# Attention and mixture-of-depths on one core: batch 2 loaded ahead of the expert weights, scatter-adds and row stores later, and matmuls of zeros at the start

## The chip, the cores and the metric

The kernel runs on one core of a Trainium2 chip. The metric is the device time of one execution in microseconds. Before the change it is 253.89 us, the median of three runs (253.05 to 253.95). The profiled execution took 251.56 us, of which 249.8 us lie between its first and its last instruction; every position in time below is counted from that first instruction.

## The reference

Two stages, for 8 batches of 448 tokens. The first is attention with a squared relu in place of the softmax, over 12 heads of 64. The second takes the 128 tokens of each batch with the highest gate score, runs them through an expert of two matrices, and adds the gated result to their rows.

```python
scores = q @ k.T / sqrt(64)                    # per batch and head, 448 x 448
x      = (maximum(scores, 0)**2 / 448) @ v     # heads side by side: 448 x 768
s      = x @ w_gate                            # per batch, 448
top    = indices of the 128 largest s
h      = maximum(x[top] @ w1, 0)               # 768 -> 1024
out    = x;  out[top] += sigmoid(s[top]) * (h @ w2)
```

Inputs and output are in fp32. Each batch of q, k and v is 4.13 MB in memory and 2.06 MB on the chip, as the loads cast to bf16.

## The kernel before

**The stages of a pair.** Work goes by pairs of heads: 8 batches of 6 pairs, 48 iterations of one loop. (b, p) is the iteration for pair p of batch b. `transposes` brings q and k of a pair into the layout that the scores need (TensorE, then a copy `qkt` by VectorE). `scores` makes four chunks of the score matrix (L186, L190), `relu` evacuates each on ScalarE (L198), `square` squares it on VectorE (L204), and `attend` multiplies by v (L214). `evacuate` writes the transposed output of the pair to `xT`, on VectorE for pairs 0, 4 and 5 and on ScalarE for the others; a DMA transpose on the SyncE queue (L229) then turns it into the columns of `x_sb`, the rows of the batch. Iteration (b, p) does the transposes of the *next* pair and attends to and evacuates the *previous* one, so the transposes for pair 0 of batch b+1 are in (b, 5), and `attend` for the last pair of batch b is in (b+1, 0).

**The expert, in the shadow of later batches.** Tables (`PE`, `ACT`, `DVE`, `DVE2`) place its steps. In batch b's iterations the tokens of batch b-1 are ranked: gate scores at pair 0, `rank_chunk` (L280) from pair 2, the one-hot matrix `hot` at pair 4, and `gather` (L296) at pair 5. One iteration later, at (b+1, 0), `chosen` writes the row indices `idx` (L306) and the gate `g`, and `gathered` copies the tokens to `xeT`. In batch b+1's iterations the expert of batch b-1 runs: `hidden` (w1, L329) at pairs 0 to 2, `project` (w2, L345) at pairs 3 and 4, `gated` (L350) writes `gye` at pairs 4 and 5. So `idx` of batch b is written at (b+2, 0), and `gye` of batch b is complete at (b+2, 5).

**Buffers.** q, k and v have three sets of buffers, used in turn: load b overwrites what batch b-3 used. `x_sb`, `idx` and `gye` have two: `idx` of batch b+2 is written over that of batch b, which the scatter-add of batch b must have read by then; `x_sb` of batch b+2 is written over that of batch b, which its store must have read.

**The order on the queues.** The loop stands in a manual schedule: each engine works its instructions off in the order in which the loop writes them. The loads, the weights, the row stores (L233) and the scatter-adds (L384) are all DMAs issued by GpSimd, one after the other on one queue, and GpSimd stands still while one of them waits to be issued. A load of a batch is nine DMAs: one for q and four each for k and v. There are eight completion semaphores for these DMAs, used in turn, so each waits at its issue for the landing of the one eight places ahead of it. The store of a batch covers rows of `out` and the scatter-add addresses all of `out`, so a scatter-add waits for the landing of a store issued ahead of it, and a store for that of a scatter-add ahead of it.

Before the change, GpSimd issues load 0, load 1, the four iotas (from which VectorE makes `slot_row`, `tie` and `tok`), w1, w2 and load 2. Then, with load(b+2) at (b, 0), the store of batch b-1 when its last pair is evacuated at (b, 0), and the scatter-add of batch b-2 at (b, 5), the order is: load 3, store 0, load 4, store 1, scatter-add 0, load 5, store 2, scatter-add 1, load 6, store 3, scatter-add 2, load 7, store 4, scatter-add 3, and from there a store and a scatter-add in turn.

Of the kernel before, what the change touches and what calls it, by code (L numbers as in the profile page):

```python
# [7 lines left out]
FP32 = mybir.dt.float32  # L8
BF16 = mybir.dt.bfloat16
# [10 lines left out]
def kernel(  # L20
# [11 lines left out]
    nc = tc.nc  # L32

    B, H, S, Dh = q.shape
# [43 lines left out]
    def load_q(b, h0, h1):  # L78
        nc.gpsimd.dma_start(
            out=q_sb[b % NBUF][:, h0:h1],  # L80
            in_=q[b, h0:h1].rearrange("h (p c) d -> p h c d", c=NC))
# [13 lines left out]
    def load(b, h0, h1):  # L95
        load_q(b, h0, h1)
        load_kv(k_sb, k, b, h0, h1)
        load_kv(v_sb, v, b, h0, h1)


    load_q(0, 0, 2)
    wg_cols = const.tile([128, NM], FP32)
    nc.sync.dma_start(out=wg_cols, in_=moe_w_gate.rearrange("(m p) -> p m", p=128))
# [11 lines left out]
    for i in range(1, NBUF):  # L115
        zero_halves(i)
    load(1, 0, H)
    w1_sb = const.tile([128, NM, F], BF16)
    w2_sb = const.tile([128, NF, HD], BF16)

    wg_rep = const.tile([128, NM, 128], BF16)
    nc.vector.tensor_copy(out=wg_rep,
# [26 lines left out]
        nc.vector.tensor_copy(out=t[:, :, 0:2], in_=tok_i)  # L149
        tok.append(t)  # L150

    nc.gpsimd.dma_start(out=w1_sb, in_=moe_w1.rearrange("(m p) f -> p m f", p=128))
    nc.gpsimd.dma_start(out=w2_sb, in_=moe_w2.rearrange("(m p) f -> p m f", p=128))


    qkt, s_ps, a_sb, o_ps, x_sb = {}, {}, {}, {}, {}
# [61 lines left out]
    def evacuate(t):  # L218
        b, hp = divmod(t, NHP)
        xt = xT[b % 2][:, hp, :, :P]  # L220
        o = o_ps.pop(t).rearrange("d (c p) -> d c p", p=P)
        if hp in (0, 4, 5):
            nc.vector.tensor_scalar(out=xt, in0=o, scalar1=o_scale, scalar2=None, op0=ALU.mult)  # L223
        else:
            nc.scalar.activation(out=xt, in_=o, func=AF.Copy, scale=o_scale)
        if hp == 0:
            x_sb[b] = x_pool.tile([128, NC, HD], BF16, name="x_sb")

        nc.sync.dma_start_transpose(  # L229
            out=x_sb[b][:, :, hp * 128:(hp + 1) * 128],  # L230
            in_=xT[b % 2][:, hp].rearrange("d c p -> d (c p)"))
        if hp == NHP - 1:
            nc.gpsimd.dma_start(out=out[b].rearrange("(p c) d -> p c d", c=NC), in_=x_sb[b][:P])  # L233

# [85 lines left out]
    def moe_ffn(b, idx, g, xeT):  # L320
        hT = moe_pool.tile([128, NF, CAP], BF16, name="hT")
        gye = moe_pool.tile([CAP, HD], FP32, name="gye")
        ps = {}

        def hidden(f, pool=mb_ps_pool, tag="m"):
            if f % 4 == 0:
                ps["h", f // 4] = pool.tile([128, 4, CAP], FP32, name="h_ps", tag=tag)
            for m in range(NM):
                nc.tensor.matmul(out=ps["h", f // 4][:, f % 4, :],  # L329
                                 lhsT=w1_sb[:, m, f * 128:(f + 1) * 128],  # L330
                                 rhs=xeT[:, m, :], start=(m == 0), stop=(m == NM - 1))

        def hidden_relu(i):
            nc.scalar.activation(out=hT[:, 4 * i:4 * i + 4, :], in_=ps["h", i], func=AF.Relu)

        def sigmoid():
            nc.scalar.activation(out=g, in_=g, func=AF.Sigmoid)

        def project(half, f0, f1, pool=None, tag="m"):
            cols_d = slice(half * 384, half * 384 + 384)  # L340
            if f0 == 0:
                pool = pool or (ma_ps_pool, mb_ps_pool)[half]
                ps["y", half] = pool.tile([CAP, 384], FP32, name="ye_ps", tag=tag)
            for f in range(f0, f1):
                nc.tensor.matmul(out=ps["y", half], lhsT=hT[:, f, :], rhs=w2_sb[:, f, cols_d],  # L345
                                 start=(f == 0), stop=(f == NF - 1))

        def gated(half):
            cols_d = slice(half * 384, half * 384 + 384)
            nc.scalar.activation(out=gye[:, cols_d], in_=ps["y", half], func=AF.Copy,  # L350
                                 scale=g[:, 0:1])
            if half == 1:
                scatter()

        def last():

            nc.scalar.activation(out=g, in_=g, func=AF.Sigmoid)
            for half in range(2):
                h = s_ps_pool.tile([128, 4, CAP], FP32, name="h_ps2", tag="s")
                for m0 in (0, 3):  # L360
                    for ff in range(4):
                        f = 4 * half + ff
                        for m in range(m0, m0 + 3):
                            nc.tensor.matmul(out=h[:, ff, :],
                                             lhsT=w1_sb[:, m, f * 128:(f + 1) * 128],
                                             rhs=xeT[:, m, :], start=(m == 0 and ff == 0),
                                             stop=(m == NM - 1), skip_group_check=True)
                f = 4 * half
                nc.scalar.activation(out=hT[:, f:f + 4, :], in_=h, func=AF.Relu)
            y = [mb_ps_pool.tile([CAP, 384], FP32, name="y_ps2", tag="m"),  # L370
                 t_ps_pool.tile([CAP, 384], FP32, name="y_ps3", tag="t")]
            for f0 in (0, 4):
                for half in range(2):
                    for f in range(f0, f0 + 4):
                        nc.tensor.matmul(out=y[half], lhsT=hT[:, f, :],
                                         rhs=w2_sb[:, f, half * 384:half * 384 + 384],
                                         start=(f == 0), stop=(f == NF - 1))
            nc.scalar.activation(out=gye[:, :384], in_=y[0], func=AF.Copy, scale=g[:, 0:1])
            nc.vector.tensor_scalar(out=gye[:, 384:], in0=y[1], scalar1=g[:, 0:1],
                                    scalar2=None, op0=ALU.mult)  # L380
            scatter()

        def scatter():
            nc.gpsimd.indirect_dma_start(  # L384
                out=out.rearrange("b s d -> (b s) d"),
                out_offset=bass.IndirectOffsetOnAxis(ap=idx[:, :1], axis=0),
                in_=gye, in_offset=None, element_offset=b * S * HD, compute_op=ALU.add)

        return {"h": hidden, "hT": hidden_relu, "sig": sigmoid, "y": project, "gye": gated,
                "last": last}  # L390


# [42 lines left out]
    with tc.manual_schedule():  # L435
        transposes(0)
        for t in range(NT):
            b, hp = divmod(t, NHP)
            scores(t, 0)
            scores(t, 1)  # L440
            relu(t, 0)
            relu(t, 1)
            moe(ACT, b, hp)
            if t > 0:
                square(t - 1, 3)
            moe(DVE, b, hp)
            if t + 1 < NT:
                transposes(t + 1)
            if t > 0:
                attend(t - 1)  # L450
                if hp not in (0, 1, 5):
                    evacuate(t - 1)
            if hp == 0 and b + 2 < B:
                load(b + 2, 0, H)
            scores(t, 2)
            relu(t, 2)
            square(t, 0)
            if t > 0 and hp in (0, 1, 5):
                evacuate(t - 1)
            square(t, 1)  # L460
            moe(DVE2, b, hp)
            scores(t, 3)
            relu(t, 3)
            square(t, 2)
            moe(PE, b, hp)
        square(NT - 1, 3)
        place(ACT, B - 1, NHP)
        place(DVE, B - 1, NHP)
        last, prev = B - 1, B - 2
        r, handed[last] = moe_rank(last)  # L470
        f = moe_ffn(prev, *handed.pop(prev))
        attend(NT - 1)
        evacuate(NT - 1)
        r["gate"](0, NM - 1)
        for i in range(4):
            f["h"](i)
        r["gate"](NM - 1, NM)
        f["hT"](0)
        r["bc"]()
        for i in range(4, 8):  # L480
            f["h"](i, t_ps_pool, "t")
        r["col"]()
        r["pieces"]()
        for c in range(NC):
            r["rank"](c)
        r["hot"]()
        f["hT"](1)
        f["sig"]()
        f["y"](0, 0, 8, mb_ps_pool)
        f["y"](1, 0, 8, o_ps_pool, "o")  # L490
        f["gye"](0)
        f["gye"](1)
        r["xe"](0, t_ps_pool, "t")
        r["sel"]()
        r["xe"](1, ma_ps_pool)
        r["xeT"](0)
        r["xeT"](1)
        r["chosen"]()
        moe_ffn(last, *handed.pop(last))["last"]()
# [33 lines left out]
```

## Time and profile before

| what | value |
|---|---|
| time, median of 3 | 253.89 us |
| span of the profiled execution | 249.8 us, mean granted TensorE clock 0.942 |
| TensorE / VectorE / ScalarE busy | 201.2 / 179.9 / 183.2 us |
| GpSimd's DMA queue (loads, weights, stores, scatter-adds) | 40768 packets, 33.82 MB, 84.4% of the span of 16 engines |
| SyncE's DMA queue (48 transposes) | 26896 packets, 6.30 MB, 25.2% |
| scatter-adds, from issue to landing | 5.5 to 7.0 us |
| row stores, from issue to landing | 5.2 to 15.7 us |
| w1, w2, from issue to landing | 17.3 and 26.1 us |

The profile's slices give the busy share of each engine in 40 equal parts of the span, in tenths. In the timelines a row is a group of instructions: start, length, engine, line, operation, what it writes and reads, and, in brackets, how long the engine had been idle before it and what ended that. The releaser is inferred from semaphores: where an instruction waits for several things, the one that came last by the profile is named. "Issue to landing" of a DMA begins when the engine issues it; it includes the time that it stands in its queue behind others. A packet's share of time includes its waiting, so the two queues together can exceed 100%.

### The profile page before, as it was taken

The numbers are of one execution on the slowest core, as the hardware profiler recorded it, in microseconds if no ns is written. First come the engines' busy times: TensorE is split into PE (matmuls) and PEld (weight loads), VectorE is DVE, ScalarE is ACT, GpSimd is POOL, SyncE is SP. The second block draws the span as 40 slices with busy tenths as digits, with TensorE's granted clock in tenths as the row PEclk, the third lists the DMA queues.
The fourth block names the chain that finished last, engine by engine and source line by source line (L and its number), as shares of the span: only waits on it lengthen the run. The fifth ranks groups of instructions, "written<-read, shape, count | busy, mean of one in ns | idle before, by whom it ended". The sixth has DMA issues, their size and how long they took to land.

```text
span 249.8 us, 5910 instructions
## 1 busy us (share of the span) xinstructions
PE 201.2 (81%) x2304; PEld 115.5 (46%) x2304; DVE 179.9 (72%) x430; ACT 183.2 (73%) x273; POOL 83.5 (33%) x117
## 2 busy tenths in 40 slices
PE   1677789730599979999999999999999499999730
PEld 0233244310265536654565456555655256456710
DVE  5274789960287979798979998998999289974300
ACT  2376989960078998899889979997999568964210
POOL 8998671101645410091101910092103012020220
PEclk9997999975589999999999999999999979999995
DMA  4999999999999999989998999999994968667443
GB/s 37 106 133 180 186 138 180 204 176 183 192 192 162 316 188 234 197 114 155 185 173 131 135 172 157 267 110 141 142 278 118 154 220 127 223 70 172 120 62 55
DMA packets 67692, 40.50 MB, mean 162 GB/s; under 512 B 40912, under 2 KB 64976, under 8 KB 66768
## 3 DMA queue, kind: packets, MB, share of 16 engines
q0 software_dynamic: 40768, 33.82, 84.4%
q1 hardware_dynamic: 26896, 6.30, 25.2%
q8 instruction: 18, 0.29, 0.5%
q14 instruction: 10, 0.08, 0.1%
HBM read 39.32 MB, written 14.16 MB: 214 GB/s over the span
## 4 chain that ended last, share of the span: by engine, by line
DMA 31%; PE 30%; ACT 12%; DVE 9%; POOL 8%; issue 6%; POOLq 1%; ACTq 0%; DVEq 0%
DMA k_sb<-in_k_dram 19%; ACT r_sb L198 9%; DMA q_sb<-in_q_dram 5%; PE s_ps L186 5%; PE o_ps L214 5%; DVE a_sb L204 4%; DMA out_dram<-x_sb 4%; PE xe_ps L296 4%; PE sc_ps L257 3%; PE h_ps L329 3%; DMA out_dram<-gye,idx 3%; PE ye_ps L345 2%; DVE trash L280 2%; PE t_ps L165 2%; PE s_ps L190 2%
## 5 line engine op out<-in xcount | busy, mean ns | idle before, releaser
L198 ACT ACTIVATE r_sb<-s_ps 128x896 bf16<-128x896 f32 x192 | 148.7, 833 | 41.9 <-PE s_ps L186 41.3
L204 DVE TENSOR_TENSOR a_sb<-r_sb 128x896 bf16<-128x896 bf16 x192 | 100.4, 559 | 10.5 <-ACT r_sb L198 9.4
L186 PE MATMUL s_ps<-qkt 64*128 64x448 bf16 x288 | 50.1, 368 | 11.4 <-ACT r_sb L198 9.3
L176 DVE COPY qkt<-t_ps 128x960 bf16<-128x960 bf16 x48 | 31.4, 654 | 31.4 <-PE t_ps L171 31.4
L214 PE MATMUL o_ps<-a_sb,v_sb 128*64 128x448 bf16 x384 | 47.7, 369 | 0.2 <-DVE a_sb L204 0.2
L384 POOL DMA_INDIRECT out_dram<-gye,idx x8 | 13.6, 1696 | 77.9 <-ACT r_sb L198 22.2
L186 PEld LDWEIGHTS <-qkt 64*128 64x128 bf16 x288 | 14.4, 94 | 46.7 <-issue 36.5
L165 PE MATMUL t_ps<-ident,q_sb 112*64 112x112 bf16 x384 | 19.6, 227 | 14.0 <-DMA q_sb<-in_q_dram 14.0
L91 POOL DMA_DIRECT2D v_sb<-in_v_dram x20 | 15.6, 780 | 42.5 <-DMA q_sb<-in_q_dram 22.8
L171 PE MATMUL t_ps<-ident,k_sb 128*64 128x128 bf16 x384 | 21.3, 230 | 6.2 <-DMA k_sb<-in_k_dram 6.2
L329 PE MATMUL h_ps<-xeT,w_sb 128*128 128x128 bf16 x336 | 22.1, 219 | 4.0 <-DVE xeT L311 3.1
L214 PEld LDWEIGHTS <-v_sb 128*64 128x64 bf16 x384 | 20.7, 115 | 9.0 <-issue 1.9
L165 PEld LDWEIGHTS <-q_sb 112*64 112x64 bf16 x384 | 12.1, 114 | 26.9 <-DMA q_sb<-in_q_dram 15.1
L329 PEld LDWEIGHTS <-w_sb 128*128 128x128 bf16 x336 | 20.4, 97 | 7.2 <-issue 5.7
L280 DVE SCALAR_TENSOR_TENSOR trash<-bc,cols,tie 112x448 bf16<-112x448 f32 x32 | 21.7, 678 | 0.1
L88 POOL DMA_DIRECT2D v_sb<-in_v_dram x20 | 17.1, 854 | 13.5 <-DMA w_sb<-in_moe_w_dram 9.0
L345 PE MATMUL ye_ps<-w_sb,hT 128*128 128x384 bf16 x112 | 20.3, 326 | 0.0
L91 POOL DMA_DIRECT2D k_sb<-in_k_dram x20 | 17.6, 885 | 2.2 <-PE s_ps L190 2.2
L190 PE MATMUL s_ps<-qkt 128*128 128x448 bf16 x48 | 17.7, 368 | 0.7 <-ACT r_sb L198 0.2
L171 PEld LDWEIGHTS <-k_sb 128*64 128x64 bf16 x384 | 14.7, 116 | 7.5 <-DMA k_sb<-in_k_dram 4.6
L88 POOL DMA_DIRECT2D k_sb<-in_k_dram x20 | 17.3, 870 | 0.2 <-issue 0.2
L223 DVE TENSOR_SCALAR xT<-o_ps 128x448 bf16<-128x448 f32 x24 | 14.8, 618 | 0.5 <-PE o_ps L214 0.5
(61 smaller groups left out, 176.1 us busy)
## 6 DMA issues: line engine op xcount, KB each, us to landing
out_dram<-x_sb POOLq DMA_DIRECT2D x8, 1344.0 KB, 10.8
q_sb<-in_q_dram POOLq DMA_DIRECT2D x7, 672.0 KB, 11.7
w_sb<-in_moe_w_dram POOLq DMA_DIRECT2D x2, 1536.0 KB, 21.7
k_sb<-in_k_dram POOLq DMA_DIRECT2D x14, 192.0 KB, 13.2
v_sb<-in_v_dram POOLq DMA_DIRECT2D x14, 192.0 KB, 10.4
k_sb<-in_k_dram POOLq DMA_DIRECT2D x14, 144.0 KB, 12.5
v_sb<-in_v_dram POOLq DMA_DIRECT2D x14, 144.0 KB, 14.2
x_sb<-xT SPq DMA_TRANSPOSE x48, 7.5
```

The costliest lines, as they stand in the source:

```text
L88: nc.gpsimd.dma_start(out=t[0:64, hs, 0:lo, :], in_=src[b, hs, 0:64 * lo].rearrange("h (p c) d -> p h c d", c=lo))
L91: nc.gpsimd.dma_start(out=t[64:128, hs, 0:hi, :], in_=src[b, hs, 64 * lo:S].rearrange("h (p c) d -> p h c d", c=hi))
L165: nc.tensor.matmul(out=ps[64 * hh:64 * hh + 64, c * P:(c + 1) * P], lhsT=qs[:, h0 + hh, c, :], rhs=ident[:P, :P], is_transpose=True, start ...
L171: nc.tensor.matmul(out=ps[64 * hh:64 * hh + 64, S + c * 128:S + (c + 1) * 128], lhsT=ks[:, h0 + hh, c, :], rhs=ident, is_transpose=True, s ...
L176: nc.vector.tensor_copy(out=sb, in_=ps)
L186: nc.tensor.matmul(out=ps[:, hh, :S], lhsT=sb[rows, S + c * 128:S + (c + 1) * 128], rhs=sb[rows, :S], start=True, stop=True)
L198: nc.scalar.activation(out=r[:, :n], in_=s_ps.pop((t, c))[:, :n, :S], func=AF.Relu)
L204: nc.vector.tensor_tensor(out=a[:, :n], in0=r[:, :n], in1=r[:, :n], op=ALU.mult)
L214: nc.tensor.matmul(out=o_ps[t][rows, :], lhsT=vs[:, 2 * hp + hh, c, :], rhs=a[:, hh if c < 3 else 0, :], start=(c == 0), stop=(c == 3), sk ...
L280: nc.vector.scalar_tensor_tensor(out=trash, in0=bc[:P, :], scalar=cols[:, c:c + 1], in1=tie[:, c, :], op0=ALU.subtract, op1=ALU.is_ge, acc ...
L329: nc.tensor.matmul(out=ps["h", f // 4][:, f % 4, :], lhsT=w1_sb[:, m, f * 128:(f + 1) * 128], rhs=xeT[:, m, :], start=(m == 0), stop=(m == ...
L345: nc.tensor.matmul(out=ps["y", half], lhsT=hT[:, f, :], rhs=w2_sb[:, f, cols_d], start=(f == 0), stop=(f == NF - 1))
```

## The change

Four edits. (1) Load 2 is issued right after load 1, and the expert weights after it, ahead of the iotas; the loop's load(b+2) then begins with load 3. It is for having batch 2 on the chip when batch 1 is done. (2) The scatter-add is taken out of `gated` and becomes a step of its own, `add`; the scatter-add of batch b-3 is issued at the end of iteration (b, 2). (3) The row store is taken out of `evacuate`; the store of batch b-1 is issued at the end of (b, 2) too, after the scatter-add. Both are for letting the loads at the start of a batch be issued without waiting behind a scatter-add. (4) 14 matmuls of zeros on TensorE while the first heads are loaded, which are to bring up its clock; they write a PSUM buffer that nothing reads.

```diff
+    blank = const.tile([128, S], BF16)
+    nc.vector.memset(blank, 0.0)
+    warm = o_ps_pool.tile([128, S], FP32, name="warm", tag="o")
+    for i in range(14):
+        nc.tensor.matmul(out=warm, lhsT=blank[:, :128], rhs=blank, start=True, stop=True)
     load_q(0, 0, 2)
...
     load(1, 0, H)
+    load(2, 0, H)
     w1_sb = const.tile([128, NM, F], BF16)
     w2_sb = const.tile([128, NF, HD], BF16)
+    nc.gpsimd.dma_start(out=w1_sb, in_=moe_w1.rearrange("(m p) f -> p m f", p=128))
+    nc.gpsimd.dma_start(out=w2_sb, in_=moe_w2.rearrange("(m p) f -> p m f", p=128))
...
-    nc.gpsimd.dma_start(out=w1_sb, in_=moe_w1.rearrange("(m p) f -> p m f", p=128))
-    nc.gpsimd.dma_start(out=w2_sb, in_=moe_w2.rearrange("(m p) f -> p m f", p=128))
...
-        if hp == NHP - 1:
-            nc.gpsimd.dma_start(out=out[b].rearrange("(p c) d -> p c d", c=NC), in_=x_sb[b][:P])
+
+    def store(b):
+        nc.gpsimd.dma_start(out=out[b].rearrange("(p c) d -> p c d", c=NC), in_=x_sb[b][:P])
...
-            if half == 1:
-                scatter()
-
...
-            if hp == 0 and b + 2 < B:
+            if hp == 0 and 2 < b + 2 < B:
                 load(b + 2, 0, H)
...
             moe(PE, b, hp)
+            if hp == 2:
+                if b >= 3:
+                    ffn_steps[b - 3]["add"]()
+                if b >= 1:
+                    store(b - 1)
...
         attend(NT - 1)
         evacuate(NT - 1)
+        ffn_steps[B - 3]["add"]()
+        store(last)
...
         f["gye"](0)
         f["gye"](1)
+        f["add"]()
```

In the order that results, GpSimd issues load 0, load 1, load 2, w1, w2, the iotas, load 3, store 0, load 4, store 1, load 5, scatter-add 0, store 2, load 6, scatter-add 1, store 3, load 7, scatter-add 2, store 4, scatter-add 3, and from there a store and a scatter-add in turn. The copies that VectorE makes from the iotas, which ran at 35.9 to 38.4 us, some pairs ahead of the ranking, stand just ahead of the first `rank_chunk`.

More of the change, by code (lines that the diff above doesn't have):

```diff
@@ L387, in scatter @@
                 in_=gye, in_offset=None, element_offset=b * S * HD, compute_op=ALU.add)
-        return {"h": hidden, "hT": hidden_relu, "sig": sigmoid, "y": project, "gye": gated,
+        return {"h": hidden, "hT": hidden_relu, "sig": sigmoid, "y": project, "gye": gated, "add": scatter,
                 "last": last}
```

## The prediction

> **What bounds the kernel now.** I read the slices of the page first, then the waits of the two stretches in which TensorE falls, then the timelines of the engines named there. The slices (6.24 us each):
>
> ```profile
> PE   1677789730599979999999999999999499999730
> ...
> PEclk9997999975589999999999999999999979999995
> DMA  4999999999999999989998999999994968667443
> ```
>
> Counted from 0, TensorE is busy nearly throughout from slice 11 (69 us) to 36, after a hole in slices 8 to 10 and with a dent in slice 31. The DMA engines are 90% busy or more in slices 1 to 29 but two. So compute and transfers each fill the middle; which of them leads is to be found stretch by stretch. The hole, in the timeline of PE:
>
> ```profile
> 52.22 0.80 PE L186 MATMUL s_ps<-qkt 64*128 64x448 bf16 x4 [0.85 <-ACT r_sb L198]
> 62.42 0.58 PE L165 MATMUL t_ps<-ident,q_sb 112*64 112x112 bf16 x8 [9.40 <-DMA q_sb<-in_q_dram]
> ...
> 66.41 0.60 PE L171 MATMUL t_ps<-ident,k_sb 128*64 128x128 bf16 x7 [1.56 <-DMA k_sb<-in_k_dram]
> ```
>
> The last pair of batch 1 wants the transposes of batch 2's first pair: TensorE is ready at 53.0 us, q lands at 62.4, k at 66.3. That is 13.4 us, and it is a wait for bytes: batch 2 stands in the GpSimd queue behind the two expert weights. The dent, in the waits between 180 and 205 us:
>
> ```profile
> DVE idx L306 <- DMA out_dram<-gye,idx: 4.5, 1, 4.5
> ```
>
> VectorE writes the indices of batch 5 into a buffer that the scatter-add of batch 3 still reads (two buffers of idx). Everything behind it on VectorE stands for 4.5 us. Where L306 runs marks the pace of the batches; the six rows are those of iterations (2,0) to (7,0):
>
> ```profile
> 71.05 0.16 DVE L306 TENSOR_TENSOR idx<-sel 128x1 int32<-128x1 f32 x1
> 97.36 0.16 DVE L306 TENSOR_TENSOR idx<-sel 128x1 int32<-128x1 f32 x1
> 121.50 0.16 DVE L306 TENSOR_TENSOR idx<-sel 128x1 int32<-128x1 f32 x1
> 145.64 0.16 DVE L306 TENSOR_TENSOR idx<-sel 128x1 int32<-128x1 f32 x1
> 169.78 0.16 DVE L306 TENSOR_TENSOR idx<-sel 128x1 int32<-128x1 f32 x1
> 198.38 0.16 DVE L306 TENSOR_TENSOR idx<-sel 128x1 int32<-128x1 f32 x1 [4.50 <-DMA out_dram<-gye,idx]
> ```
>
> A batch of compute takes 24.14 us; the last interval is 24.14 plus the wait; from 198.38 to the end (249.8) are 51.4 us. Against that, the transfers, from the GpSimd timeline:
>
> ```profile
> 91.57 0.55 POOL L233 DMA_DIRECT2D out_dram<-x_sb  x1
> 105.60 1.69 POOL L384 DMA_INDIRECT out_dram<-gye,idx  x1 [13.48 <-DVE a_sb L204]
> ...
> 136.54 1.71 POOL L384 DMA_INDIRECT out_dram<-gye,idx  x1 [16.05 <-ACT xT L225]
> ...
> 162.73 1.66 POOL L384 DMA_INDIRECT out_dram<-gye,idx  x1 [11.49 <-ACT r_sb L198]
> ...
> 191.34 2.10 POOL L384 DMA_INDIRECT out_dram<-gye,idx  x1 [10.73 <-ACT r_sb L198]
> ```
>
> The engine named as releaser had long been done: each scatter-add waits for the landing of the store ahead of it. Store 1 is issued at 91.57, takes 13.1 us to land (104.6), and scatter-add 0 follows. The round of load, store, scatter-add thus takes 30.9, 26.2 and 28.6 us, longer than a batch of compute. The transfers lose ground until they stop VectorE at 198 us.
>
> **What the Trainium skill says.** "DMA: Bandwidth & Descriptors", section "Queues, rings and completion order": each DMA engine goes round-robin between its queues, a packet at a time. The trace agrees: with no transposes the load of a batch moves at 198 GB/s (86.3 to 89.5 us); between 91 and 98 us the GpSimd queue and the transpose queue have 1902 and 1883 packets, and the load gets 0.81 MB in 7 us, 116 GB/s. Same page, "Two DMAs through the same engine are not ordered": within one queue descriptors start in order. The trace agrees: a store alone lands in 5.2 to 5.8 us, store 2, issued behind a load, in 15.7. "TensorE: Matmul & The Clock Gate", "Part 1": after an idle window of about 3.4 us TensorE runs at half clock. Here the granted clock is 0.55 from 66.4 to 71 us, and 0.57 from 200 to 202, after the 4.5 us wait.
>
> **The change, part by part.** *Load 2 ahead of the weights.* From the landing of load 1 (last piece issued at 27.39, 9.4 us to land: 36.8) the queue moves w1, w2 and load 2 without a gap until load 2's last piece lands (62.66 and 7.3: 69.9). Only their order changes. Load 2 at 198 GB/s is 2.06 MB / 0.198 = 10.4 us and some three transposes beside it, so it is there at about 50 us, w1 at 60, w2 at 70. The 13.4 us wait goes. First use of w1 (L329) comes some 7 us into batch 2, about 63 us; of w2 (L345) about 76: no wait. *New wait on VectorE.* The iotas now stand on GpSimd behind both weight issues, which wait for the semaphores of the first two k pieces of load 2 (about 43.5 and 44.5 us). The copies from the iotas now stand on VectorE just ahead of the first ranking, reached about 43.7 us before; tie_i (1.66 us on GpSimd) is ready near 47.3. Some 3.6 us, with squares and qkt copies queued behind. *The zeros.* 14 matmuls of at most 0.37 us (L186's mean) at full clock, double at half clock: 5 to 10 us in the first load, whose transposes run at 4.6 us before; bounds 0 and +5 us, taken at 2. Net, batch 2 starts some 9 us earlier than at 66.4, and (4,0) is reached at about 121.5 - 9.5 = 112 us instead of 121.5.
>
> *Scatter-adds later.* This decides. Scatter-add 0 moves from ahead of load 5 to behind it. Its reader comes at (4,0), where idx of batch 2 is written into the same buffer. And the transfers are not earlier: up to store 1 they are the same bytes in the same order but for the weights, back to back, so store 1 still lands near 104.6; the DMA row falls off at about 103.5, its last data. Then load 5: 10.4 us; each transpose beside it costs it 7 x (198 - 116) / 198 / 3.5 = 0.83 us (0.46 MB are 3.5 transposes), six of them 5.0; together 15.4. From the rounds of before I get the same term with its disturbances: round less 3.7 us (store landed to first scatter data), 2.8 (scatter data), 4.3 (store): 20.1, 15.4, 17.8. The first held a store colliding with transposes; five transposes rather than six stand ahead at (4,0). I take 16.4, bounds 15.4 and 20.1. Then 2.8 for the scatter-add and 0.7 to its receipt: 103.5 + 16.4 + 3.5 = 123.4 us. So VectorE waits at (4,0) from 112 to 123.4, about 11 us, and arrives 1.9 us later than before: the first wait is moved, not removed.
>
> From there (5,0), (6,0), (7,0) follow at 24.14 us each by compute, plus 0.4 for the cold clock (from L306 to the one-hot takes 19.07 us after the wait at 198 us, 18.72 elsewhere): 147.9, 172.1, 196.2. The transfers: store 2 behind scatter-add 0, 4.8 us; load 6, 16.4; scatter-add 1, 3.5: 148.1, and again 172.8. Level with compute, costing some 0.7. (7,0) finds scatter-add 3 landed, since no loads are left: 184 by the same terms. So (7,0) is at 196.9 against 198.38, the 4.5 us wait gone; the tail starts warm, 0.3 less. Sum: -1.5 - 0.3 = -1.8 us, less what near ties cost on top, 0.4: -1.4.
>
> *Stores later.* They free GpSimd from waiting at the batch's start, and x_sb is then reused later: the transposes of batch 4 wait for store 2 (about 129 us), and gathering needs them at (5,5), about 166. Hidden.
>
> **Rivals.** (a) Transfer-bound from (4,0) on. If loads take 17.8 us as in the third round, scatter-add 0 lands at 124.8 and the next ones 26.1 us apart, 150.9 and 177.0; (7,0) is then at 201.2, 2.8 later, so 256.5; at 20.1 us a load it is 262. For it: two of three rounds were so long. Against: the one disturbed most held a collision which no longer occurs, as store 2 now comes when batch 3's transposes are done. (b) The full gain: 9.5 us of earlier start and 4.5 at (7,0), 240. It needs the queue to run ahead, and the DMA row has no spare slice. (c) Level: scatter-add 0 at about 125, so the gain at (7,0) is just spent: 253.9.
>
> **How the numbers follow.** Forecast 253.9 - 1.4 = 252.5, chance 0.56; (a) 0.27; (b) 0.06; (c) 0.11. The forecast's spread (load 15.4 gives -3.4) lies about three quarters beyond -1.27 us (0.5%): faster 0.42 + 0.06 = 0.48. Same: 0.14 + 0.11 + 0.02 from (a). Slower 0.25. The range, 250.2 to 258, leaves (b) and the worse third of (a) out.
>
> **What the new profile would show.** Right: no hole near 60 us; VectorE waiting some 3 us for GpSimd near 45; an idx wait of 8 to 14 us near 112 to 124, by far the longest on VectorE; L306 24 to 25.5 us apart after that; no idx wait at (7,0). Wrong: if the idx waits at (5,0) and (6,0) are several us each, it is (a). If store 1 lands well before 103 us, the back-to-back queue was wrong, and the gain is larger.

## The result, and the profile after

The changed kernel takes 269.19 us (median of four runs, 266.56 to 270.63), against 253.92 us (253.05 to 254.8) for the kernel before: a ratio of 1.0567, with a 95% interval of 1.0477 to 1.0657. The forecast was 252.5, with a range up to 258. A ratio, here and below, compares only the runs of each kernel that lie within 1.5% of its fastest, so it can differ from the ratio of the medians, which are of all runs. The profiled execution has a span of 266.9 us, against 249.8, and a mean granted clock of 0.885, against 0.942.

The slices of the profile after, 6.67 us each:

```profile
PE   7589787689979999570099989997499999999750
PEclk9855999889999999955579999999689999999795
DMA  4999999999999999999499999999659177147424
```

The 14 matmuls of zeros show at the left edge. The hole of before at 53 to 66 us is gone. In its place stands a new one in the middle, where TensorE is idle and its clock falls to half, and the DMA row now has a gap there too (slice 19). What VectorE writes into `idx` dates both. These are the rows of VectorE's timeline for iterations (2,0) to (7,0), with the idle time ahead of each in brackets (L314 is L306 of before):

```profile
61.27 0.16 DVE L314 TENSOR_TENSOR idx<-sel 128x1 int32<-128x1 f32 x1
86.68 0.16 DVE L314 TENSOR_TENSOR idx<-sel 128x1 int32<-128x1 f32 x1
132.03 0.16 DVE L314 TENSOR_TENSOR idx<-sel 128x1 int32<-128x1 f32 x1 [21.26 <-DMA out_dram<-gye,idx]
159.63 0.16 DVE L314 TENSOR_TENSOR idx<-sel 128x1 int32<-128x1 f32 x1 [2.87 <-DMA out_dram<-gye,idx]
189.63 0.16 DVE L314 TENSOR_TENSOR idx<-sel 128x1 int32<-128x1 f32 x1 [6.76 <-DMA out_dram<-gye,idx]
214.60 0.16 DVE L314 TENSOR_TENSOR idx<-sel 128x1 int32<-128x1 f32 x1
```

VectorE is at (4,0) at 132.03 - 21.26 = 110.8 us, 10.7 earlier than before (121.50). There it waits 21.3 us for scatter-add 0, and starts 10.5 us later than before. Two more waits follow at (5,0) and (6,0). The wait of 4.5 us at (7,0) is gone, but (7,0) comes at 214.6 instead of 198.4. So nearly all of the loss of 17.1 us of span has come by (7,0), and it arises after (3,0), which was still 10.7 us earlier than before (86.68 against 97.36). The waits of the whole run (engine, what it needed, what ended the wait; total us, times, longest) say how it spreads. The last row is from the profile of before:

```profile
POOL out_dram L241 <- DMA out_dram<-gye,idx: 35.9, 4, 11.3
DVE idx L314 <- DMA out_dram<-gye,idx: 30.9, 3, 21.3
PE h_ps L337 <- DVE xeT L319: 21.2, 3, 14.3
...
POOL out_dram L233 <- DMA out_dram<-gye,idx: 9.3, 2, 5.1
```

The third line is TensorE behind VectorE: one wait, seen one engine on. In the first line GpSimd stands before a *store* until a *scatter-add* has landed. Before, that was 9.3 us, all of it in the tail, where no load is left; now 20.9 of the 35.9 us come in the middle, before stores that have a load queued behind them. GpSimd's timeline shows what that does to the order (L241 store, L389 scatter-add, L88 a piece of a load):

```profile
91.08 0.55 POOL L241 DMA_DIRECT2D out_dram<-x_sb  x1 [0.66 <-DMA k_sb<-in_k_dram]
112.50 0.66 POOL L88 DMA_DIRECT2D v_sb<-in_v_dram  x1 [1.94 <-DMA out_dram<-x_sb]
119.24 1.69 POOL L389 DMA_INDIRECT out_dram<-gye,idx  x1 [1.60 <-ACT r_sb L205]
132.23 0.61 POOL L241 DMA_DIRECT2D out_dram<-x_sb  x1 [11.30 <-DMA out_dram<-gye,idx]
148.59 1.88 POOL L389 DMA_INDIRECT out_dram<-gye,idx  x1 [0.78 <-ACT r_sb L205]
160.09 0.58 POOL L241 DMA_DIRECT2D out_dram<-x_sb  x1 [9.62 <-DMA out_dram<-gye,idx]
177.20 1.93 POOL L389 DMA_INDIRECT out_dram<-gye,idx  x1 [1.01 <-DVE a_sb L211]
189.83 0.59 POOL L241 DMA_DIRECT2D out_dram<-x_sb  x1 [10.70 <-DMA out_dram<-gye,idx]
```

Store 1 is issued at 91.08, as before (91.57), and has landed by 112.2 (21.1 us); before it took 13.1. The second row shows it: a piece of load 5 waits for the semaphore of that store. Scatter-add 0 is issued at 119.24 behind load 5 and lands at 131.9, then store 2 is issued, and only behind it load 6. From there each round is a strict row: scatter-add lands, store, load, scatter-add. Scatter-adds 1 and 2 land at 159.5 and 189.5 us, 27.6 and 30.0 us after the one before.

Two stretches of the same run (length; busy time of PE, PEld, DVE, ACT, POOL; granted clock; DMA share; GB/s):

```profile
98.00:112.30 14.30, 12.01 (x141) 6.50 (x138) 11.71 (x28) 11.83 (x20) 1.97 (x3) 1.00 1.61 145
112.30:132.00 19.70, 4.88 (x35) 2.06 (x36) 0.00 (x0) 3.45 (x5) 3.00 (x3) 0.52 1.24 141
```

In the second, VectorE does nothing at all, and the granted clock is 0.52. This agrees with what the Trainium skill says in "TensorE: Matmul & The Clock Gate", "Part 1": half clock after an idle window. The first is the riddle: DMA engines that are busy all the time move 145 GB/s while a store is on its way. Here are the packets of the stretch in which store 1 moves. Before, 98 to 102 us:

```profile
DMA packets 641, 1.50 MB, mean 374 GB/s; under 512 B 234, under 2 KB 536, under 8 KB 536
q0 software_dynamic: 473, 1.46, 112.6%
q1 hardware_dynamic: 168, 0.03, 8.2%
```

After, 98 to 112 us:

```profile
DMA packets 1948, 2.03 MB, mean 145 GB/s; under 512 B 1025, under 2 KB 1836, under 8 KB 1836
q0 software_dynamic: 967, 1.76, 90.0%
q1 hardware_dynamic: 978, 0.24, 70.3%
```

q0 is the queue of loads, stores and scatter-adds, q1 that of the transposes. 1948 - 1836 = 112 packets are of 8 KB or more, nearly all of them store 1's (1344 KB, in packets of 12 KB). Before, 105 such packets went through in 4 us, as hardly a transpose was under way. After, they share 14 us with 978 transpose packets and with some 855 small ones of q0, the end of load 4. A transpose packet took, its waiting included, 0.703 x 16 x 14 / 978 = 0.16 us there, against 0.082 x 16 x 4 / 168 = 0.03 us before. The two queues move one packet for one (967 and 978), which agrees with the Trainium skill ("DMA: Bandwidth & Descriptors", "Queues, rings and completion order": round-robin, a packet at a time). By turns alone, though, a large packet should lose little to a small one: at 0.03 us each, 978 transpose packets on 16 engines are an estimated 978 x 0.03 / 16 = 1.8 us of the 14. Why the total falls to 145 GB/s the page doesn't say, and no run here shows it.

### The profile page after: what moved, and what is told of

Same layout as the page of the kernel before. It is cut to its first block, busy times and chain, and to the rows that moved or that the text cites. A ratio compares the mean times of both kernels' runs of the same rounds, so it can differ in the third digit from the quotient of the medians.

```text
span 266.9 us, 5938 instructions
## 1 busy us (share of the span) xinstructions
PE 211.5 (79%) x2318; PEld 119.1 (45%) x2318; DVE 180.7 (68%) x431; ACT 183.1 (69%) x273; POOL 82.8 (31%) x117
## 4 chain that ended last, share of the span: by engine, by line
PE 31%; DMA 30%; DVE 13%; ACT 10%; issue 7%; POOL 6%; POOLq 1%; ACTq 0%; DVEq 0%
DMA k_sb<-in_k_dram 16%; DMA out_dram<-gye,idx 13%; ACT r_sb L205 7%; PE s_ps L193 6%; DVE a_sb L211 5%; PE o_ps L221 5%; PE sc_ps L265 4%; PE h_ps L337 3%; PE xe_ps L304 3%; DVE trash L288 2%; PE t_ps L172 2%; PE t_ps L178 2%; DVE qkt L183 1%; PE h_ps L369 1%; POOL q_sb L79 1%
## 5 line engine op out<-in xcount | busy, mean ns | idle before, releaser
L211 DVE TENSOR_TENSOR a_sb<-r_sb 128x896 bf16<-128x896 bf16 x192 | 100.2, 559 | 11.6 <-ACT r_sb L205 10.6
L193 PE MATMUL s_ps<-qkt 64*128 64x448 bf16 x288 | 51.6, 382 | 10.6 <-ACT r_sb L205 8.8
L221 PE MATMUL o_ps<-a_sb,v_sb 128*64 128x448 bf16 x384 | 48.6, 376 | 1.8 <-DVE a_sb L211 1.8
L337 PEld LDWEIGHTS <-w_sb 128*128 128x128 bf16 x336 | 20.8, 99 | 25.7 <-issue 24.5
L91 POOL DMA_DIRECT2D v_sb<-in_v_dram x20 | 13.5, 676 | 51.1 <-DMA q_sb<-in_q_dram 14.7
L389 POOL DMA_INDIRECT out_dram<-gye,idx x8 | 13.4, 1679 | 47.3 <-DVE a_sb L211 17.3
L178 PE MATMUL t_ps<-ident,k_sb 128*64 128x128 bf16 x384 | 20.9, 230 | 2.6 <-DMA k_sb<-in_k_dram 2.6
L314 DVE TENSOR_TENSOR idx<-sel 128x1 int32<-128x1 f32 x8 | 1.3, 159 | 31.1 <-DMA out_dram<-gye,idx 30.9
L172 PE MATMUL t_ps<-ident,q_sb 112*64 112x112 bf16 x384 | 19.9, 230 | 0.5 <-DMA q_sb<-in_q_dram 0.5
L88 POOL DMA_DIRECT2D v_sb<-in_v_dram x20 | 13.6, 682 | 21.6 <-DMA w_sb<-in_moe_w_dram 8.5
L241 POOL DMA_DIRECT2D out_dram<-x_sb x8 | 4.6, 577 | 48.5 <-DMA out_dram<-gye,idx 35.9
L304 PE MATMUL xe_ps<-hot,x_sb 112*128 112x128 bf16 x192 | 13.5, 223 | 5.4 <-DMA x_sb<-xT 3.3
L232 ACT ACTIVATE xT<-o_ps 128x448 bf16<-128x448 f32 x24 | 13.3, 553 | 6.6 <-PE o_ps L221 6.6
```

The lines of the kernel that those rows point to most:

```text
L172: nc.tensor.matmul(out=ps[64 * hh:64 * hh + 64, c * P:(c + 1) * P], lhsT=qs[:, h0 + hh, c, :], rhs=ident[:P, :P], is_transpose=True, start ...
L178: nc.tensor.matmul(out=ps[64 * hh:64 * hh + 64, S + c * 128:S + (c + 1) * 128], lhsT=ks[:, h0 + hh, c, :], rhs=ident, is_transpose=True, s ...
L193: nc.tensor.matmul(out=ps[:, hh, :S], lhsT=sb[rows, S + c * 128:S + (c + 1) * 128], rhs=sb[rows, :S], start=True, stop=True)
L211: nc.vector.tensor_tensor(out=a[:, :n], in0=r[:, :n], in1=r[:, :n], op=ALU.mult)
L221: nc.tensor.matmul(out=o_ps[t][rows, :], lhsT=vs[:, 2 * hp + hh, c, :], rhs=a[:, hh if c < 3 else 0, :], start=(c == 0), stop=(c == 3), sk ...
L304: nc.tensor.matmul(out=xe[:, mm, :], lhsT=xb[:P, c, m * 128:(m + 1) * 128], rhs=hot[:, c, :], start=(c == 0), stop=(c == NC - 1))
```

## The experiments

Theory A, from the trace: the loss is the scatter-add standing behind a load, so that `idx` isn't free at (4,0). Theory B: the early load or the zeros do harm by themselves. Theory C, the way in which the expectation of the first experiment lets B work, later tested by itself: store 1 is late because it meets transposes already under way. Kernels that ran together shared the runs of the kernel before: medians 254.96, 252.79, 255.38 and 253.06 us in the four groups, with single runs from 246 to 265, so intervals are wide.

**Each half alone.** `e1_loads_only` is the changed kernel with store and scatter-add in their old places:

```diff
...
+        if hp == NHP - 1:
+            nc.gpsimd.dma_start(out=out[b].rearrange("(p c) d -> p c d", c=NC), in_=x_sb[b][:P])
...
+            if half == 1:
+                scatter()
...
-            if hp == 2:
-                if b >= 3:
-                    ffn_steps[b - 3]["add"]()
-                if b >= 1:
-                    store(b - 1)
...
```

> The changed kernel with scatter-adds and stores where they were before (load 2 ahead of the weights, and the zeros, stay). Theory A (the scatter-add behind a load, read against two buffers of idx, costs the time): scatter-add 0 is again ahead of load 5 and lands some 7 us after store 1, at 112 to 119; the idx wait at (4,0) is 2 to 8 us instead of 21; later rounds are as before the change, so 250 to 256 us. Theory B (starting batch 2 early makes its transposes run into store 1, which lands 7.6 us later, and everything behind it): the 7.6 us stay in the chain of transfers to the end: 260 to 264 us.

Measured: 255.15 us, ratio 1.0176 [0.9967, 1.0385]. (4,0) at 118.77, (7,0) at 198.52, with four idx waits of 10.9 us together. The total is A's, not B's: no harm of the early load by itself shows, and no gain, as the lead is eaten by (7,0). But store 1 is as late here as B says. It is issued at 88.68 and lands at 109.4, and GpSimd stands for it before scatter-add 0 (the releaser named had long been done), with no load queued behind the store. The stretch in which it moves, in GpSimd's row and the window (columns as above):

```profile
110.40 1.69 POOL L391 DMA_INDIRECT out_dram<-gye,idx  x1 [21.17 <-DVE a_sb L211]
...
98.00:106.00 8.00, 7.86 (x100) 4.87 (x98) 7.44 (x21) 7.58 (x14) 0.00 (x0) 1.00 1.30 148
```

`e2_later_only` is the reverse, the kernel before with those later places alone (the same lines the other way round).

> The kernel before with only the scatter-adds and stores moved half a batch later. Theory A: scatter-add 0 lands some 21 us after store 1 (104.6), at 125 to 127, against an idx write at 121.5; then rounds of 27 to 30 us: (7,0) at 207 to 210, 262 to 265 us. Theory B: batch 2 does not start early, store 1 lands at 104.6, so close to before: 254 to 258 us.

Measured: 255.67 us, ratio 1.017 [1.0095, 1.0245]. The 262 to 265 us that A gave is missed, and the 254 to 258 of B met: alone, the later places cost little, 1.7% by the ratio and 0.7 us between the medians. Its windows say why; here a load is under way at first, and store 1 after it (columns as above):

```profile
90.00:98.00 8.00, 7.84 (x92) 4.41 (x92) 5.93 (x14) 5.65 (x9) 3.82 (x6) 0.86 1.41 186
98.00:102.20 4.20, 4.17 (x51) 2.15 (x47) 3.33 (x7) 3.61 (x7) 1.97 (x3) 1.00 1.15 366
```

Store 1 goes through at 366 GB/s, and the piece of load 5 that waits for it is issued at 103.09, against 112.50 after. Scatter-add 0 follows behind load 5, and `idx` is written at 122.82, just after VectorE gets there (idx wait 1.4 us, then 4.4 at (5,0)). From that piece to `idx` it takes 19.7 us, against 19.5 after (112.50 to 132.03). So the later scatter-add alone meets a late reader and a quick store; with batch 2 early, the reader is 10.6 us earlier (110.8 against 121.4) and the store 9.4 later. A load queued behind store 1 isn't what makes it late: e2 has one and e1 has none. Only both edits together lose 15 us.

**The zeros.** `e4_no_zeros` leaves the memset and the 14 matmuls out of the changed kernel.

> The changed kernel without the 14 matmuls of zeros. Both theories: batch 2's start is hidden in the idx wait at (4,0), so within 2 us of the changed kernel, 267 to 271 us. If the zeros cost or bring something that is not hidden, it differs by more than that.

Measured: 265.98 us, ratio 1.0581 [1.0243, 1.0918]; the idx wait at (4,0) is 21.3 us as with them. At the start the trace shows what they do: with them the first eight transposes of q take 0.39 us and the first scores start at 7.49 us, without them 0.58 and 8.18. Of that nothing can be told later: (2,0) is at 60.65 instead of 61.27, but at 62.7 to 64.0 in other runs with the zeros. So neither the zeros nor, in e1, the early load loses the 15 us by itself, and the 260 to 264 us that B gave for e1 fall. What it says of store 1 stands.

**The wait for idx.** `e3_idx_gye_4` takes the reason of the wait away:

```diff
+    deep = ctx.enter_context(tc.tile_pool(name="deep", bufs=4))
...
-        idx = small.tile([CAP, 1], INT32, name="idx")
+        idx = deep.tile([CAP, 1], INT32, name="idx")
...
-        gye = moe_pool.tile([CAP, HD], FP32, name="gye")
+        gye = deep.tile([CAP, HD], FP32, name="gye")
```

> The changed kernel with four buffers of idx and gye instead of two, so that no index is written over one that a scatter-add has still to read. Theory A: the three idx waits (30.9 us) go; (4,0) at 110.6, then 24.1 us a batch unless a load is late (load 5 landed at 130.3, wanted from about 130 on): (7,0) at 183 to 190, so 236 to 243 us. Theory B: the queue is late by itself and loads set the pace: 258 us or more.

Measured: 256.47 us (249.85 to 262.15), 12.7 less than after, but not the 236 to 243 of A. In the profiled run (256.54) no idx wait is left, and (7,0) comes at 188.40, as A had it. But from there to the end it takes 66.4 us instead of 52.3: the time returns in the tail. Its waits, and GpSimd's timeline of the tail:

```profile
POOL out_dram L242 <- DMA out_dram<-gye,idx: 56.1, 6, 14.4
```

```profile
192.31 0.59 POOL L242 DMA_DIRECT2D out_dram<-x_sb  x1 [14.41 <-DMA out_dram<-gye,idx]
198.37 1.69 POOL L390 DMA_INDIRECT out_dram<-gye,idx  x1 [5.47 <-ACT r_sb L206]
205.12 0.58 POOL L242 DMA_DIRECT2D out_dram<-x_sb  x1 [5.07 <-DMA out_dram<-gye,idx]
212.72 1.60 POOL L390 DMA_INDIRECT out_dram<-gye,idx  x1 [7.02 <-DVE trash L289]
```

A store, a scatter-add, a store, each issued when the one before has landed. Compute has been freed, and the chain of the output sets the end.

`e11_no_scatter` is e3 without any scatter-add.

> The kernel of e3 (the changed one with four buffers of idx and gye) with the scatter-adds left out, so that the experts' rows are not added to the output. If e3's end was set by stores and scatter-adds waiting for each other: (7,0) at 184 to 188, 51 to 52 us to the end, 238 to 243 us. If it was set by loads or stores themselves: 250 us or more.

Measured: 246.58 us, ratio 0.9688 [0.9392, 0.9983]. The median is 9.9 us under that of e3: about what the scatter-adds still cost once nothing waits for idx. Two runs (241.86 and 242.78) are in the first range of the expectation, two (250.38 and 251.21) in the second. Even in the profiled one (242.78) the gaps before (5,0) and (6,0) are 26.7 and 29.7 us, with TensorE waiting for `x_sb`: without any scatter-add, the transfers still hold up compute there.

**The place behind the load.** `e7_add_before_load` moves only the scatter-add, from the end of (b, 2) to (b, 0):

```diff
+            if hp == 0 and b >= 3:
+                ffn_steps[b - 3]["add"]()
             if hp == 0 and 2 < b + 2 < B:
                 load(b + 2, 0, H)
...
-                if b >= 3:
-                    ffn_steps[b - 3]["add"]()
```

> The changed kernel with one line moved: the scatter-add of batch b-3 is issued at (b, 0) ahead of load(b+2) instead of at (b, 2) behind it; stores stay at (b, 2). Theory A: scatter-add 0 lands some 7 us after store 1, at 112 to 119; the idx wait at (4,0) is 2 to 8 us instead of 21, the total 250 to 257 us. If it is not the place behind the load that counts: 264 us or more.

Measured: 256.7 us, ratio 1.0268 [1.0084, 1.0452], 12.5 less than after; each of its runs (252.86 to 258.31) is below each of the changed kernel's. VectorE's rows for (4,0) to (7,0):

```profile
122.52 0.16 DVE L314 TENSOR_TENSOR idx<-sel 128x1 int32<-128x1 f32 x1 [4.21 <-DMA out_dram<-gye,idx]
147.98 0.16 DVE L314 TENSOR_TENSOR idx<-sel 128x1 int32<-128x1 f32 x1 [2.21 <-DMA out_dram<-gye,idx]
174.28 0.16 DVE L314 TENSOR_TENSOR idx<-sel 128x1 int32<-128x1 f32 x1 [3.05 <-DMA out_dram<-gye,idx]
199.51 0.16 DVE L314 TENSOR_TENSOR idx<-sel 128x1 int32<-128x1 f32 x1 [1.99 <-DMA out_dram<-gye,idx]
```

Store 1 is as late as in the changed kernel (113.9; GpSimd stands 24.5 us before the scatter-add for it). With no load between, `idx` is written at (4,0) 9.5 us earlier, and no wait after that exceeds 3.1. The wait there falls by more, from 21.3 to 4.2, because VectorE arrives only at 118.3; 5.0 us of that is a gap on TensorE at 111 to 116 us that ends in nothing the profile shows.

**Why store 1 is late.** `m1_store_turns` and `m2_load_store_turns` only issue loads, stores and transposes of the kernel's sizes; each was run once.

> No attention and no expert: only the DMAs in question, with pauses between: a store alone; three transposes alone; a store with three transposes beside it; a load alone; a load with six transposes; a load and a store behind it, with six transposes that are still under way when the store comes. The output is zeros. Theory C (transposes beside a store are dear for both): the store alone takes 5 to 6 us from issue to landing, with three transposes 9 us or more; the load alone about 11 us of data, with six transposes 15 to 16. Against C: packets only take turns, so three transposes (1.1 us each alone) add at most 3.5 us to the store.

A store alone took 5.18 us, and 5.18 with three transposes begun behind it; a load 14.3, with six transposes 17.9. In the last form, load and store, the transposes were issued 3.9 us after the store and came too late to meet it: 17.5 us in all, the store 3.4 after the load's last piece. Transposes that begin only when the store's data flow don't slow it: these forms speak against C.

> No attention and no expert, zeros as output: a store alone; a load and a store behind it; the same with six transposes begun some 6 us after the load, so that about three are left when the store comes; the same with a second load behind the store. Theory C (a store is dear when transposes are already under way): without transposes the store lands 3.5 to 4.5 us after the load's last piece, with them 8 us or more after it. Against C: at most 2 us more than without, as packets only take turns.

m2 has the transposes under way when the store's turn comes. Load and store without transposes: 17.65 us, 3.2 of them after the load's last piece. With six transposes begun 6 us into the load: 25.1; with another load behind: 25.8. From the first experiment, load with transposes and then the store should take 17.9 + 3.2 = 21.1, so the meeting costs 4 to 4.7 us. By the sign set for it, though, C fails: the store landed 2.9 and 3.1 us after the load's last piece, not 8 or more. What came late with it was the end of the load, whose last two pieces landed 4.4 and 4.1 us after the piece before, instead of 0.8 and 1.0 without transposes. The windows of m2, first the load and the store without transposes, then the load and the store with them (busy times of DVE and POOL alone, as no other engine computes):

```profile
55.15:69.60 14.45, 11.39 (x5) 6.79 (x10) 1.00 1.23 182
69.60:72.80 3.20, 2.69 (x1) 0.00 (x0) 1.00 0.65 253
86.95:104.00 17.05, 13.73 (x6) 6.78 (x10) 1.00 1.29 157
104.00:112.00 8.00, 6.68 (x2) 0.00 (x0) 1.00 1.26 167
```

The last row is the meeting: 167 GB/s for the end of the load, the store and the transposes together. So C holds in a wider form: it's not the store alone that slows, but all that moves while a store's large packets meet transposes under way. The changed kernel shows the same picture. The transposes of batch 2 are made early, all wait for store 0 (`x_sb` has two buffers), and are issued in one row from 85.7 to 93.4 us. Three of them have not landed when store 1's data come at 98; they land at 101.5, 109.2 and 113.6. The last two pieces of load 4 land at 103.9 and 109.6 (before: 99.4 and 100.3), and the store 2.6 us after them. `e5_after_x3` gives `x_sb` three buffers, so that they need not wait:

```diff
-    x_pool = ctx.enter_context(tc.tile_pool(name="x", bufs=2))
+    x_pool = ctx.enter_context(tc.tile_pool(name="x", bufs=3))
```

> The changed kernel with three buffers of x_sb, so that the transposes of batch 2 need not wait for store 0 and are made one by one, beside load 3. Theory C: none of them is left when store 1 moves, which lands at 102 to 106 instead of 112.2, scatter-add 0 at 121 to 126, the idx wait at (4,0) is 11 to 15 us instead of 21, total 258 to 263 us. Against it (the queue is late because compute and its transposes are early at all): store 1 at 108 or later, total 266 to 270.

Measured: 267.35 us, from four runs of 263.31, 263.66, 271.04 and 273.67. In the profiled one (263.31) store 1 lands at 107.9, 13.7 us from its issue instead of 21.1, and scatter-add 0 at 126.4 instead of 131.9: over half of the way. The idx wait at (4,0) falls further, to 11.1 us, because VectorE also gets there 4.7 us later; 2.7 and 7.8 us follow at (5,0) and (6,0). The span of this run, 261.5 us, is 5.4 less than after, as much as scatter-add 0 gained. But the four runs spread too far to say that the kernel is faster.

`e14_after_x1` goes the other way. With `bufs=1` the transposes of a batch can't start before the store of the batch before has landed.

> The changed kernel with one x_sb buffer: the transposes of a batch start only when the store of the batch before has landed and its gather is done. Meeting theory: store 1 lands at 102 to 105 us instead of 112.2, the idx wait at (4,0) is under 15 us instead of 21.3, and the kernel takes less than 262 us. Rival (the transfers alone set the pace): store 1 lands after 108, the wait stays above 18 us, 266 us or more.

Measured: 269.66 us, ratio 1.0702 [1.0626, 1.0777]. The first half of the expectation is met: store 1 is issued at 95.08, the stretch moves 286 GB/s, and the piece of load 5 that waits for the store is issued at 102.14, against 112.50 after:

```profile
95.00:100.10 5.10, 5.10 (x44) 2.49 (x43) 2.83 (x5) 3.45 (x5) 4.91 (x8) 0.69 0.86 286
```

At (4,0) `idx` is written at 124.44, 7.6 us earlier than after. The wait for it is only 3.6, since VectorE gets there at 120.9, ten microseconds later. The second half fails: not a microsecond is won. TensorE now waits for the transposes that had to start later, 7.7 us in five waits between 90 and 126 us; from its timeline:

```profile
118.98 0.83 PE L304 MATMUL xe_ps<-hot,x_sb 112*128 112x128 bf16 x12
121.18 0.40 PE L304 MATMUL xe_ps<-hot,x_sb 112*128 112x128 bf16 x4 [1.28 <-DMA x_sb<-xT]
124.20 1.23 PE L304 MATMUL xe_ps<-hot,x_sb 112*128 112x128 bf16 x8 [2.63 <-DMA x_sb<-xT]
```

The same edit on the kernel before (`e12_before_x1`), on that with four idx and gye buffers (`e15_before_x1_idx4`), and on e6 below (`e13_e6_x1`):

> The kernel before with one x_sb buffer. Meeting theory: no store is slowed; store 1 lands 5 to 8 us after its issue instead of 13.1, the idx wait of 4.5 us at (5,0) of before is gone, 245 to 252 us. Rival (transfers alone, or the tighter chain of store, transposes and gather costs more): a new wait for x or idx, 254 us or more.

> The kernel before with four idx and gye buffers and one x_sb buffer. Meeting theory: no idx wait, stores land 5 to 8 us after issue, 244 to 250 us. Rival: the wait moves from idx to x (gathers after a store), 253 us or more.

> Early loads, scatter-adds and stores in their old places, four idx and gye buffers, one x_sb buffer. Meeting theory: stores land 5 to 8 us after their issue, the chain of stores and scatter-adds of the tail shortens, 242 to 248 us. Rival (transfers set the pace, each batch's store, load and gather now in a strict row): rounds over 25 us and 252 us or more.

Measured: 259.88, 260.42 and 261.02 us, ratios 1.0296 [1.0203, 1.0389], 1.0342 [1.027, 1.0413] and 1.0358 [1.0287, 1.0428]. In all three the stores land in 5.1 to 7.7 us once the first is over, and no idx wait is left (the one of before stands at (7,0), not at (5,0)). All three are slower than before, and TensorE waits 7.6, 8.1 and 10.9 us for `x_sb`: the rival won. Meeting a store is one price of transposing beside it; not meeting it has another.

**The rounds after scatter-add 0.** `e10_after_own_rows` narrows what the scatter-add is declared to touch, so that the next store need not wait for it:

```diff
-                out=out.rearrange("b s d -> (b s) d"),
+                out=out[0:b + 1].rearrange("b s d -> (b s) d"),
```

> The changed kernel with each scatter-add addressing only the rows of out up to its own batch, so that a store of a later batch no longer waits for it, nor it for such a store. Theory A: scatter-add 0 still stands behind load 5, so the idx wait at (4,0) stays near 21 us; store 2 no longer waits for it to land, which saves some 3 to 5 us of each later round, so the waits at (5,0) and (6,0) go: (7,0) at 204 to 208 instead of 214.6, 256 to 261 us. If those waits between stores and scatter-adds cost nothing: 265 to 270.

Measured: 262.12 us (258.21 to 266.30), ratio 1.0394 [0.9963, 1.0824]. In the profiled run, the longest, GpSimd no longer waits for a scatter-add before a store. The one idx wait left is at (4,0), 26.0 us: the piece that waits for store 1 is issued 4.3 us later than in the changed kernel, and scatter-add 0 takes 16.0 us from its issue, with store 2 issued right behind it, instead of 12.7. From there (5,0), (6,0) and (7,0) follow 24.8, 24.1 and 24.1 us apart. So it takes the strict row of scatter-add, store and load to make the 27.6 and 30.0 us rounds of the changed kernel.

**A better kernel?** `e6_loads_idx4` puts e1 and the four buffers together, and `e8_e6_own_rows` adds the narrowed scatter-add.

> The kernel of e1 (load 2 ahead of the weights, the zeros, scatter-adds and stores in their old places) with four buffers of idx and gye. Theory A: its four idx waits (10.9 us together) go, (7,0) at 187 to 190 instead of 198.5; then the stores and scatter-adds, each waiting for the one before, set the end: 244 to 250 us. If the loads set the pace: 252 to 256.

> The kernel of e6 (load 2 early, zeros, old places, four buffers of idx and gye) with scatter-adds that address only the rows up to their own batch. If the chain of stores and scatter-adds set e6's end: (7,0) at 187 to 189 as in e6, then 51 to 52 us instead of 60 to the end, 240 to 245 us. If bytes of loads, stores and transposes set it: 250 us or more.

Measured: 253.51 us, ratio 1.0098 [0.9932, 1.0263], and 255.65 us, 1.0196 [0.995, 1.0442]. In e6 (7,0) comes at 188.77, 9.6 us earlier than before, and an unbroken chain of stores and scatter-adds from 192.7 to 246.1 gives it all back; before, that chain ran from 191.3 to 246.9. In e8 that chain is loosened, but stores 1 to 4 land 18.7 to 24.9 us after issue, TensorE waits for `x_sb` (7.8 us), and (7,0) comes only at 196.50: the rival of its expectation, 250 us or more. None of these runs beats the kernel before.

## Why the prediction was wrong

**What held.** No hole near 60 us. The first wait "is moved, not removed": (4,0) is reached at 110.8 (said: 112) and stands there for idx, by far the longest wait on VectorE, though 21.3 us and not 8 to 14. No idx wait at (7,0). From the landing of store 1 to that of scatter-add 0, behind load 5, it took 19.7 us; the working had 18.8 (104.6 to 123.4).

**The small terms.** The new wait for the iotas, some 3.6 us, did not come: `slot_row` is cast at 46.24 us, directly behind a square that ran to the same moment. The zeros, taken at 2 us, cost nothing that e4 can tell. These errors favour the change, and were lost in the wait that follows. One sum of the rivals is off: by its own terms a load of 20.1 us gives about 263, not 262.

**The step that failed first** is "up to store 1 they are the same bytes in the same order but for the weights, back to back, so store 1 still lands near 104.6". The bytes and their order on GpSimd's queue were the same, and load 4's pieces came as before up to 97.9 us. What differed was the other queue: the transposes of batch 2, early now, stood in a bunch behind store 0, and the last two pieces of load 4 and store 1 met them. It landed at 112.2. Against the predicted 123.4, scatter-add 0 came at 131.9: 8.5 us, 7.6 of them from store 1. That such a meeting slows the whole stretch, m2 shows with nothing else under way; that store 1 is late with the early load and quick without it, e1 and e2 show. e2 also shows that without the meeting the later places cost little. That removing the meeting alone would save these 8.5 us isn't shown: e5 removed over half of it, and gained as much in the one run profiled; e14 removed it, and gave the time back elsewhere. The working knew that stores collide with transposes, and said that this "no longer occurs" for store 2; it wasn't asked for store 1, and among its signs is one for a store 1 that comes early, none for one that comes late.

**The second failed term** is the load of 16.4 us in the rounds, "store 4.8 + load 16.4 + 3.5", 24.7 and so level with compute. Between the landings of scatter-adds 0, 1 and 2 the stores took 5.3 us from issue. From the landing of the store to that of the next scatter-add, where the sum had 16.4 + 3.5 = 19.9, it took 22.0 and 24.1 us; with the bound of 20.1 it would have been 23.6. The sum had the row strict, one transfer after the other, and so it is: load 6 is issued only when scatter-add 0 has landed and store 2 has been issued, and nothing of it moves during the 11.3 us for which GpSimd waits. e10 takes that wait away, and the rounds are 24 to 25 us. Why the loads took longer than 16.4 stays open. Here the Trainium skill asks for care: it says ("DMA: Bandwidth & Descriptors", "Rules for kernel authors") that an accumulating DMA beside another access of the same bytes needs a semaphore wait. The store of another batch touches other bytes; it waited only because the scatter-add was declared over all of `out`.

**The sum.** 8.5 (scatter-add 0) + 2.9 (round 1) + 5.3 (round 2) + 0.8 ((6,0) to (7,0), 24.97 instead of 24.14) + 1.2 (tail, 52.3 instead of 51.1) = 18.7, against 266.9 - 248.4 = 18.5 us of span. What happened is rival (a), "transfer-bound from (4,0) on", by its own sign: idx waits of several us at (5,0) and (6,0). It had been given 256.5 to 262, since it too began from store 1 at 104.6.

**Where the gain went.** Batch 2 early brings VectorE to (4,0) 10.7 us earlier in the changed kernel, some 6 in e1, e3 and e6. In the changed kernel it became the idx wait; in e1, four small ones; in e3 and e6, where nothing waited for idx any more, time in the tail, where the output's chain of stores and scatter-adds set the end.

## What to carry to other kernels

Before a DMA is put behind another on a queue, find its reader and the wait that the reader stands in: a scatter-add behind a load cost little while the reader came late (1.7% by the ratio, 0.7 us between medians), and 12.5 us once an earlier batch brought the reader forward. An edit that moves compute forward also moves the DMAs that compute issues on *other* queues; "the same bytes in the same order" on one queue says nothing of when they land. And after taking one wait away, look at the tail before counting it: in e6 a gain of ten microseconds in the middle was given back there in full.

## What the runs showed of the hardware

A store of 1344 KB in 12 KB packets lands 5.2 to 6.1 us after issue when nothing is ahead of it (5.18 in m1, 5.16 to 6.11 for stores 2 to 7 of the changed kernel). With hardly a transpose under way, the stretch in which a store moves runs at 366 to 374 GB/s in e2 and before, at 286 in e14 and 253 in m2. With transposes already under way, all that moves there slows: the stretch runs at 145 GB/s in the changed kernel, 148 in e1 and 167 in m2, and a transpose packet takes 0.16 us, its waiting included, instead of 0.03. Transposes that begin once the store's packets flow don't slow it (5.18 us in m1). Why the total falls when they meet stays open.
